# Decay counted from the start of each chunk of 128 tokens, the first unit's block loaded in three parts, and another PSUM bank for a 32-row step

## The chip, the cores and the metric

The kernel runs on one core of one Trainium2 chip. The metric is device time in microseconds, the median of three runs. Engines are called by their roles: TensorE (PE in the profile, PEld for its weight loads), VectorE (DVE), ScalarE (ACT), GpSimd (POOL), and SyncE (SP), which issues most of the DMAs. A kernel has one instruction queue for each engine, and each queue runs in order.

## The reference

Three layers follow each other. The first is retention: for batch 4, 8 heads, 576 tokens and 64 columns a head, with a decay gamma of its own for each head.

```python
scores = scale * np.matmul(q, k.transpose(0, 1, 3, 2))
gamma = 1.0 - 2.0 ** (-5.0 - np.arange(H))
Dmat = np.where(rel >= 0, gamma ** rel, 0.0)      # rel = row - column
out = np.matmul(scores * Dmat, v)
```

Its 2304 rows of 512 columns go through a mixture of 8 experts (512 to 1024, ReLU, 1024 to 512; each row to the expert with the largest gate logit, with a capacity), and its output through a second mixture of 8 experts, where rows whose skip score is not positive are passed on unchanged. All of it is float32.

## The kernel before

**Attention** (`attention`, from L137) works in 20 units: for each batch four units of two heads with the first 512 tokens, and a fifth (`tail`) with the last 64 tokens of all heads. Because gamma to the power of (row - column) is a product of a power for the row and one for the column, the queries are multiplied by gamma^row / 8 (`prep_q`, tile `qT`) and the values by gamma^-column (`prep_v`, tile `vh`). A main unit is four chunks of 128 tokens. Within a chunk the scores S = k q (`scores`, L219) are masked by a triangle on VectorE (`P`, L222) and multiplied by `vh` into the output O (`pv`, L263). What earlier chunks give comes through a state: `state` (L231) multiplies keys and `vh` of each chunk into one PSUM tile `kv`, whose pool has one buffer. ScalarE copies the first chunk's part (L239) and VectorE adds the other three one after another (L237). `inter` (L249) multiplies the queries with the state of the chunks before. The decay is counted from the start of the sequence, so the tables of queries have 576 columns for each pair of heads (tile `qt`): 128 are loaded, and ScalarE makes the others from them (`powers`, L205). For the first two units VectorE makes `qT` in four steps (L195, L198) from those 128. GpSimd makes `qT` of the others (L193), all `vh` but the first (L183), and both of the tails (L190, L181). The pool of `qT` and that of `vh` have three buffers.

**Order.** `round_(u)` puts the parts of neighbouring units together: prepare unit u + 1, a background slot, `inter(u - 1)`, a slot, `scores(u)`, `pv(u - 1)`, a slot, `state(u + 1)`, and the load of unit u + 5. TensorE runs in the order in which the code names the work, and from round 1 on GpSimd does too. In the first stretch, up to the end of round 0, VectorE and ScalarE also keep the written order; what is left, and VectorE, ScalarE and SyncE from round 1 on, is ordered by a planner, which simulates the program when it is built. The slots take the work of `tokens_out`: for a finished batch the gate logits (L346, copied out of PSUM at L348), their transposes `Lt` (L359), the router's chain of small VectorE operations with one exponential on ScalarE (L361 to L396, L449 to L481), the transposes of rows (L663) and their copies (L664). In the list of batch 1, `pick_first` (its count matmul `pf` is L502) chooses the expert that layer 1 begins with. GpSimd scatters the rows with indirect DMAs (L493).

**The loads.** SyncE issues them. For unit 0 these are keys and queries (512 KB), the 128 query columns of all pairs (256 KB), 56 table columns (28 KB), the keys and values by tokens (512 KB) and 260 more table columns (130 KB). Units 1 to 3 have one load of 1 MB each; the rest of the table follows unit 3. Five main blocks fit at once.

**The expert layers** come behind. First products (h, pool `psH` of two banks) are put through ReLU, and second products are summed over eight steps in four banks `y0` to `y3`. In layer 2, where the planner orders TensorE alone, an entry of 32 rows (`small1`, `small2`) works between entries 0 and 2. It sums its outputs `ys` (L903) in bank `y3`, which VectorE empties for entry 0 (L956), and ScalarE copies them out (`hold`, L1132).

Of the kernel before, what the change touches and what calls it, by code (L numbers as in the profile page):

```python
# [53 lines left out]
TAB0, TAB1 = 56, 316  # L54
# [6 lines left out]
def host_tables():  # L61
    gam = 1.0 - 2.0 ** (-5.0 - np.arange(H, dtype=np.float64))
    p = np.arange(128)
    vtab = np.zeros((128, 4, 5, 2))
    for h in range(H):
        for t in range(5):
            vtab[:, h // 2, t, h % 2] = gam[h] ** (-(128.0 * t + p))
    own = lambda j: np.repeat(gam[2 * j:2 * j + 2], 64)[:, None]
    qrow = np.stack([own(j) ** np.arange(128.0) / 8.0 for j in range(4)], axis=1)
    qg = np.stack([own(j) ** (128.0 * np.arange(1, 5)) for j in range(4)], axis=1)  # L70
    vtl = np.stack([[[gam[4 * j + 2 * a + h] ** (-(512.0 + t)) for h in range(2)] for a in range(2)] for j in range(2) for t in range(64)])
    one = np.ones((128, 1))
    cols = {
        "vtab": vtab.reshape(128, 40),
        "qg": qg.reshape(128, 16),
        "tri": p[:, None] <= p[None, :],
        "tri2": (p[:, None] <= p[None, :]) & (p[:, None] // 64 == p[None, :] // 64),
# [18 lines left out]
    return {"tab": np.ascontiguousarray(tab), "qrow": np.ascontiguousarray(qrow.astype(np.float32))}, off  # L96
# [40 lines left out]
def attention(g, hooks):  # L137
# [13 lines left out]
    def load(u):  # L151
# [10 lines left out]
        part = lambda c0, c1: nc.sync.dma_start(out=g.tab[:, c0:c1], in_=g.ia["tab"][:, c0:c1])  # L162
        if u == 0:
            nc.sync.dma_start(out=x[:, 0:1024], in_=src[:, 0:1024])
            nc.sync.dma_start(out=g.qt[:, :, 0:128], in_=g.ia["qrow"])
            part(0, TAB0)
            nc.sync.dma_start(out=x[:, 1024:], in_=src[:, 1024:])
            part(TAB0, TAB1)
        else:
            nc.sync.dma_start(out=x, in_=src)  # L170
        if u == 3:
            part(TAB1, g.tab.shape[1])
            g.small_loads()
        elif u == 10:
            g.clear(1)

    def prep_v(u):
        s = st[u]
        s.vh = g.wk.tile([128, 4, 2, DH], F32, tag="vh", name=f"vh{u}", bufs=3)
        if tail(u):  # L180
            nc.gpsimd.tensor_mul(s.vh[:, 0:2], s.v, g.vtl[:, :, :, None].to_broadcast([128, 2, 2, DH]))  # L181
        else:
            (nc.gpsimd if u else nc.vector).tensor_mul(s.vh, s.v, g.vtab[:, s.p, 0:4, :, None].to_broadcast([128, 4, 2, DH]))  # L183

    def prep_q(u):

        s = st[u]
        s.qT = g.wk.tile([128, 512], F32, tag="qT", name=f"qT{u}", bufs=3)
        if tail(u):
            nc.gpsimd.tensor_mul(s.qT[:, 0:256].rearrange("p (a j t) -> p a j t", a=2, j=2), s.q.rearrange("p (a j t) -> p a j t", a=2, j=2),  # L190
                                 g.qt[:, :, 512:576].rearrange("p (j a) t -> p a j t", a=2))
        elif u > 1:
            nc.gpsimd.tensor_mul(s.qT, s.q, g.qt[:, s.p, 0:512])  # L193
        else:
            nc.vector.tensor_mul(s.qT[:, 0:128], s.q[:, 0:128], g.qt[:, s.p, 0:128])  # L195
            for c in range(1, 4):
                cs = slice(128 * c, 128 * c + 128)
                nc.vector.scalar_tensor_tensor(out=s.qT[:, cs], in0=s.q[:, cs], scalar=g.qg[:, s.p, c - 1:c], in1=g.qt[:, s.p, 0:128],  # L198
                                               op0=ALU.mult, op1=ALU.mult)

    def powers(p):

        for c in range(1, 5):
            w = 128 if c < 4 else 64
            nc.scalar.activation(g.qt[:, p, 128 * c:128 * c + w], g.qt[:, p, 0:w], AF.Copy, scale=g.qg[:, p, c - 1:c])  # L205
# [18 lines left out]
    def state(u):  # L224
# [8 lines left out]
        s.st = [g.st3[main.index(u) % 2][:, c] for c in range(3)] + [g.st4[s.b % 2][:, s.p]]  # L233
        for c in range(4):
            x = kv[:, DH * c:DH * c + DH]
            if c:
                nc.vector.tensor_add(s.st[c], s.st[c - 1], x)  # L237
            else:
                nc.scalar.copy(s.st[c], x)  # L239
# [79 lines left out]
    with g.tc.manual_schedule(engines={T.PE, T.DVE, T.Activation}):  # L319
        prep_q(0)  # L320
        prep_v(0)
        scores(0)
        state(0)
        prep_q(1)
        prep_v(1)
        powers(2)
        powers(3)
        round_(0)
        powers(0)
        powers(1)  # L330
# [292 lines left out]
def tokens_out(g, b):  # L623
# [48 lines left out]
    if b == 1:  # L672
        return [logits, choose, rows[0], rows[1], g.r1.pick_first, rows[2], step, rows[3], rows[4], puts, lambda: g.puts.append(g.first)]
# [124 lines left out]
class Layer:  # L798
# [98 lines left out]
    def small2(self, pos, f, w):  # L897

        g, s = self.g, self.st[pos]
        if f == 0:  # L900
            s.y = [g.psY.tile([128, 512], F32, tag="y3", name=f"ys{pos}")[:, 0:128]]
# [523 lines left out]
def build(nc, tc, ia, oa, off, stage=99):  # L1425
# [4 lines left out]
    with ExitStack() as ctx:  # L1430
# [7 lines left out]
        tab = cp.tile([128, tw], F32, name="tab")  # L1438
# [6 lines left out]
        for n_, (o0, o1) in off.items():  # L1445
            setattr(g, n_, tab[:, o0:o1])
        g.tid1 = g.rid[:, 0:NT]
        g.vtab = g.vtab.rearrange("p (a t h) -> p a t h", a=4, t=5)
        g.qg = g.qg.rearrange("p (a c) -> p a c", a=4)
        g.vtl = g.vtl.rearrange("p (a h) -> p a h", a=2)  # L1450
# [40 lines left out]
        with ExitStack() as ac:  # L1491
# [9 lines left out]
            g.qt = ap.tile([128, 4, 576], F32, name="qt")  # L1501
# [11 lines left out]
            g.st3 = [ap.tile([128, 3, DH], F32, name=f"st3_{i}") for i in range(2)]  # L1513
# [50 lines left out]
```

## Time and profile before

| | us |
|---|---|
| median of 3 runs | 524.47 (523.34 to 529.84) |
| the profiled execution | 523.61 |
| its span, first to last instruction | 521.7 |
| TensorE busy | 498.2 |
| VectorE busy | 288.0 |
| ScalarE busy | 213.8 |
| GpSimd busy | 142.8 |

The span is shorter than the time of the execution by what lies around it. An engine counts as busy while an instruction of its own runs; waiting, branching and issuing DMAs do not count. A wait is put down to what ended it, written with an arrow.

### The profile page before, as it was taken

How to read it: one execution, taken by the hardware profiler on the slowest of the kernel's cores; microseconds unless marked ns; L12 is line 12 of the kernel's file. 1: busy time of each engine (PE TensorE's matmuls, PEld its weight loads, DVE VectorE, ACT ScalarE, POOL GpSimd, SP SyncE). 2: the span in 40 equal slices, each digit the busy share in tenths (PEclk: the TensorE clock that was granted, in tenths of full speed). 3: DMA queues.
4: the chain of work that ended last, by engine and by line, in shares of the span. 5: the costliest groups of instructions: out<-in, count | busy, mean ns of one | idle time of the engine just before them, and what ended most of it. 6: DMA issues, size and time to landing. Idle time of an engine off the chain costs nothing.

```text
span 521.7 us, 11984 instructions
## 1 busy us (share of the span) xinstructions
PE 498.2 (95%) x4411; PEld 464.2 (89%) x4411; DVE 288.0 (55%) x840; ACT 213.8 (41%) x432; POOL 142.8 (27%) x210
## 2 busy tenths in 40 slices
PE   7999798999999999999999999999999999999993
PEld 6877676798999999999999899999899889999992
DVE  4655748445365856667585857453657665522012
ACT  2332133324354746556474756332534524321120
POOL 1657465331222030412014150513110320110111
PEclk9999899999999999999999999999999999999997
DMA  8979664946997457584848563607869999988800
GB/s 308 405 231 383 211 173 155 323 134 187 297 287 229 137 166 204 190 229 132 244 128 252 162 223 123 174 11 195 283 207 298 323 302 270 290 269 274 288 24 33
DMA packets 90920, 114.15 MB, mean 219 GB/s; under 512 B 15685, under 2 KB 65861, under 8 KB 88933
## 3 DMA queue, kind: packets, MB, share of 16 engines
q1 hardware_dynamic: 84517, 99.23, 62.9%
q0 software_dynamic: 6336, 14.07, 7.2%
q8 instruction: 36, 0.59, 0.5%
q14 instruction: 31, 0.25, 0.2%
HBM read 97.99 MB, written 20.17 MB: 226 GB/s over the span
## 4 chain that ended last, share of the span: by engine, by line
PE 74%; DMA 10%; DVE 7%; issue 3%; SPq 2%; ACT 2%; POOL 1%; POOLq 0%; DVEq 0%; ACTq 0%
PE h L858 13%; PE y L934 9%; PE h L869 5%; PE h L870 5%; PE h L868 5%; PE y L938 5%; PE y L939 5%; PE y L937 5%; PE O L263 3%; PE S L219 3%; DMA rows<-xs 2%; PE y L931 2%; DMA xb<-xs 2%; PE yr L979 2%; PE O L249 2%
## 5 line engine op out<-in xcount | busy, mean ns | idle before, releaser
L786 DVE TENSOR_TENSOR lo<-r,hi 128x1024 fp32r<-128x1024 f32 x80 | 97.7, 1223 | 51.1 <-ACT hi L786 48.6
L786 ACT CAST hi<-r 128x1024 fp32r<-128x1024 f32 x80 | 83.6, 1047 | 35.6 <-PE y L938 20.1
L938 PE MATMUL y<-hl,hi 128*128 128x316 f32 (+7 forms) x256 | 76.3, 299 | 1.0 <-DVE hl L874 1.0
L939 PE MATMUL y<-hh,lo 128*128 128x316 f32 (+7 forms) x256 | 76.0, 298 | 0.0
L937 PE MATMUL y<-hh,hi 128*128 128x316 f32 (+7 forms) x256 | 74.8, 297 | 0.0
L493 POOL DMA_INDIRECT xs<-x2s,idx x20 | 23.3, 1164 | 166.9 <-DVE hl L874 46.9
L934 PE MATMUL y<-hh,r 128*128 128x176 f32 (+3 forms) x384 | 60.3, 300 | 0.0
L873 ACT ACTIVATE hh<-h 128x316 fp32r<-128x316 f32 (+8 forms) x72 | 29.2, 406 | 70.7 <-PE h L870 70.7
L934 PEld LDWEIGHTS y<-hh,r 128*128 128x128 f32 x384 | 55.0, 190 | 0.0
L874 DVE SCALAR_TENSOR_TENSOR hl<-h,hh 128x316 fp32r<-128x316 f32 (+8 forms) x72 | 32.3, 448 | 37.7 <-ACT hh L873 37.6
L938 PEld LDWEIGHTS y<-hl,hi 128*128 128x128 f32 x256 | 48.2, 188 | 1.6 <-DVE hl L874 1.6
L939 PEld LDWEIGHTS y<-hh,lo 128*128 128x128 f32 x256 | 48.3, 188 | 0.0
L937 PEld LDWEIGHTS y<-hh,hi 128*128 128x128 f32 x256 | 47.7, 188 | 0.2
L865 ACT ACTIVATE hh<-h 128x176 f32<-128x176 f32 (+3 forms) x48 | 14.6, 305 | 77.1 <-PE h L858 74.5
L1138 POOL DMA_INDIRECT out<-o,oi x13 | 16.7, 1285 | 101.8 <-DVE o L1213 69.8
L956 DVE COPY yt<-y 128x176 f32<-128x176 f32 (+11 forms) x28 | 10.5, 391 | 44.3 <-ACT yt L958 26.5
L222 DVE TENSOR_TENSOR P<-S,tab 128x512 f32<-128x512 f32 (+1 forms) x40 | 23.8, 632 | 13.5 <-PE S L219 13.4
L274 ACT COPY xT<-O 128x512 f32<-128x512 f32 x16 | 9.3, 584 | 35.2 <-PE O L263 35.2
L1138 POOL DMA_INDIRECT out<-x2r,si x20 | 21.3, 1066 | 6.1 <-issue 5.2
L858 PE MATMUL h<-x_0h,r 128*128 128x160 f32 (+1 forms) x128 | 22.7, 312 | 0.0
L219 PE MATMUL S<-qT,m 64*128 64x128 f32 x256 | 20.0, 295 | 2.4 <-DVE qT L195 1.6
L263 PE MATMUL O<-P,vh 128*64 128x128 f32 x288 | 21.9, 296 | 0.0
(617 smaller groups left out, 1183.7 us busy)
## 6 DMA issues: line engine op xcount, KB each, us to landing
r<-w1a SPq DMA_DIRECT2D x32, 512.0 KB, 4.9
r<-w2a SPq DMA_DIRECT2D x32, 512.0 KB, 5.6
r<-w1b SPq DMA_DIRECT2D x32, 512.0 KB, 5.9
r<-w2b SPq DMA_DIRECT2D x32, 512.0 KB, 5.6
m<-main SPq DMA_DIRECT2D x15, 1024.0 KB, 11.1
xb<-xs SPq DMA_DIRECT2D x12, 160.0 KB, 5.2
rows<-xs SPq DMA_DIRECT2D x7, 258.0 KB, 3.7
xb<-xs SPq DMA_DIRECT2D x12, 144.0 KB, 4.4
```

The source lines that it names most:

```text
L219: nc.tensor.matmul(S[hh][:, c], s.kT[hp, cs], s.qT[hp, cs], start=True, stop=True)
L263: nc.tensor.matmul(s.O[64 * hh:64 * hh + 64, 128 * c:128 * c + 128], s.vh[:, c, hh], s.P[:, hh, c], start=False, stop=True, skip_group_che ...
L786: high, low = lambda: nc.scalar.copy(hi, raw), lambda: nc.vector.tensor_sub(lo, raw, hi.bitcast(F32))
L858: nc.tensor.matmul(ps, w.r1[:, c, fc], s.xh[:, c, 0:C], start=(c == 0), stop=(c == 3))
L868: nc.tensor.matmul(ps, w.hi1[:, c, fc], s.xh[:, c, 0:C], start=(c == 0), stop=False)
L873: nc.scalar.activation(s.hh[f], ps, AF.Relu)
L874: nc.vector.scalar_tensor_tensor(out=s.hl[f], in0=ps, scalar=0.0, in1=s.hh[f].bitcast(F32), op0=ALU.max, op1=ALU.subtract)
L934: nc.tensor.matmul(y, w.r2[:, f % 2, dc], s.hh[f], start=a, stop=o)
L937: nc.tensor.matmul(y, wh, s.hh[f], start=a, stop=False)
L938: nc.tensor.matmul(y, wh, s.hl[f], start=False, stop=False)
L939: nc.tensor.matmul(y, wl, s.hh[f], start=False, stop=o)
L1138: r = g.nc.gpsimd.indirect_dma_start(out=g.oa["out"][:, :].rearrange("n (b d) -> (n b) d", b=parts), out_offset=IndirectOffsetOnAxis(ap=id ...
```

## The change

The decay is counted from the start of each chunk. `vh` of a main unit is the value times gamma^-p with p the row in its chunk, the same for all four chunks, so it has one scale a row and head: two ScalarE instructions, one a head, make it. `qT` takes the same 128 table columns for each chunk, in one product on VectorE (units 0 and 1) or GpSimd; `powers` and its ScalarE instructions go. The state is carried from chunk to chunk with gamma^128: ScalarE copies all four parts of `kv` out of PSUM times gamma^128 (tile `w`), and VectorE makes `state * gamma^128 + w` three times, in SBUF alone. The tail's product of queries becomes two.

Unit 0's block is loaded as queries, a first table part (268 columns with `vtab`, `g128`, the first pair's query columns and the triangle), keys, keys and values by tokens, and a second table part of 516 columns. The query table `qrow` is no longer a tensor of its own. In batch 1's list `pick_first` comes after four rows and no longer after two. `ys` is summed in a bank of the pool `psH`.

```diff
@@ -51,7 +51,7 @@
 GATE, TOK, VAL = 512, 513, 514
-TAB0, TAB1 = 56, 316
+TAB0, TAB1 = 268, 784
 F32_MAX = 192
@@ -61,19 +61,18 @@
     p = np.arange(128)
-    vtab = np.zeros((128, 4, 5, 2))
-    for h in range(H):
-        for t in range(5):
-            vtab[:, h // 2, t, h % 2] = gam[h] ** (-(128.0 * t + p))
     own = lambda j: np.repeat(gam[2 * j:2 * j + 2], 64)[:, None]
-    qrow = np.stack([own(j) ** np.arange(128.0) / 8.0 for j in range(4)], axis=1)
-    qg = np.stack([own(j) ** (128.0 * np.arange(1, 5)) for j in range(4)], axis=1)
-    vtl = np.stack([[[gam[4 * j + 2 * a + h] ** (-(512.0 + t)) for h in range(2)] for a in range(2)] for j in range(2) for t in range(64)])
+    qrow = np.stack([own(j) ** np.arange(128.0) / 8.0 for j in range(4)], axis=1).reshape(128, 512)
+    g128 = np.concatenate([own(j) ** 128.0 for j in range(4)], axis=1)
+    vtab = gam[None, :] ** (-p[:, None])
+    vtl = np.stack([[[gam[4 * j + 2 * a + h] ** (-float(t)) for h in range(2)] for a in range(2)] for j in range(2) for t in range(64)])
     one = np.ones((128, 1))
     cols = {
-        "vtab": vtab.reshape(128, 40),
-        "qg": qg.reshape(128, 16),
+        "vtab": vtab,
+        "g128": g128,
+        "qrow0": qrow[:, 0:128],
         "tri": p[:, None] <= p[None, :],
+        "qrows": qrow[:, 128:],
         "tri2": (p[:, None] <= p[None, :]) & (p[:, None] // 64 == p[None, :] // 64),
@@ -93,7 +92,7 @@
     tab = np.concatenate([c_.astype(np.float32) for c_ in cols.values()], axis=1)
-    return {"tab": np.ascontiguousarray(tab), "qrow": np.ascontiguousarray(qrow.astype(np.float32))}, off
+    return {"tab": np.ascontiguousarray(tab)}, off
@@ -159,17 +158,17 @@
         s.k, s.v = (x[:, o:o + 512].rearrange("p (c h d) -> p c h d", c=4, h=2) for o in (1024, 1536))
-        part = lambda c0, c1: nc.sync.dma_start(out=g.tab[:, c0:c1], in_=g.ia["tab"][:, c0:c1])
+        part = lambda c0, c1: nc.sync.dma_start(out=g.ta[:, c0:c1], in_=g.ia["tab"][:, c0:c1])
         if u == 0:
-            nc.sync.dma_start(out=x[:, 0:1024], in_=src[:, 0:1024])
-            nc.sync.dma_start(out=g.qt[:, :, 0:128], in_=g.ia["qrow"])
-            part(0, TAB0)
-            nc.sync.dma_start(out=x[:, 1024:], in_=src[:, 1024:])
+            for c0, c1 in ((512, 1024), (0, 512), (1024, 2048)):
+                nc.sync.dma_start(out=x[:, c0:c1], in_=src[:, c0:c1])
+                if c0 == 512:
+                    part(0, TAB0)
             part(TAB0, TAB1)
         if u == 3:
-            part(TAB1, g.tab.shape[1])
+            nc.sync.dma_start(out=g.tab, in_=g.ia["tab"][:, TAB1:])
             g.small_loads()
@@ -180,29 +179,20 @@
         else:
-            (nc.gpsimd if u else nc.vector).tensor_mul(s.vh, s.v, g.vtab[:, s.p, 0:4, :, None].to_broadcast([128, 4, 2, DH]))
+            for hh in range(2):
+                nc.scalar.activation(s.vh[:, :, hh], s.v[:, :, hh], AF.Copy, scale=g.vtab[:, 2 * s.p + hh:2 * s.p + hh + 1])
         if tail(u):
-            nc.gpsimd.tensor_mul(s.qT[:, 0:256].rearrange("p (a j t) -> p a j t", a=2, j=2), s.q.rearrange("p (a j t) -> p a j t", a=2, j=2),
-                                 g.qt[:, :, 512:576].rearrange("p (j a) t -> p a j t", a=2))
-        elif u > 1:
-            nc.gpsimd.tensor_mul(s.qT, s.q, g.qt[:, s.p, 0:512])
+            for j in range(2):
+                nc.gpsimd.tensor_mul(*(x[:, 0:256].rearrange("p (a j t) -> p a j t", a=2, j=2)[:, :, j] for x in (s.qT, s.q)),
+                                     g.qtail[j])
         else:
-            nc.vector.tensor_mul(s.qT[:, 0:128], s.q[:, 0:128], g.qt[:, s.p, 0:128])
-            for c in range(1, 4):
-                cs = slice(128 * c, 128 * c + 128)
-                nc.vector.scalar_tensor_tensor(out=s.qT[:, cs], in0=s.q[:, cs], scalar=g.qg[:, s.p, c - 1:c], in1=g.qt[:, s.p, 0:128],
-                                               op0=ALU.mult, op1=ALU.mult)
-
-    def powers(p):
-
-        for c in range(1, 5):
-            w = 128 if c < 4 else 64
-            nc.scalar.activation(g.qt[:, p, 128 * c:128 * c + w], g.qt[:, p, 0:w], AF.Copy, scale=g.qg[:, p, c - 1:c])
+            (nc.gpsimd if u > 1 else nc.vector).tensor_mul(s.qT.rearrange("p (c t) -> p c t", c=4), s.q.rearrange("p (c t) -> p c t", c=4),
+                                                           g.qrow[s.p][:, None, :].to_broadcast([128, 4, 128]))
@@ -230,13 +220,11 @@
                                  start=True, stop=True, skip_group_check=True)
-        s.st = [g.st3[main.index(u) % 2][:, c] for c in range(3)] + [g.st4[s.b % 2][:, s.p]]
-        for c in range(4):
-            x = kv[:, DH * c:DH * c + DH]
-            if c:
-                nc.vector.tensor_add(s.st[c], s.st[c - 1], x)
-            else:
-                nc.scalar.copy(s.st[c], x)
+        w, gm = g.wk.tile([128, 4, DH], F32, tag="kv", name=f"kvs{u}", bufs=3), g.g128[:, s.p:s.p + 1]
+        s.st = [w[:, 0]] + [g.st3[main.index(u) % 2][:, c] for c in range(2)] + [g.st4[s.b % 2][:, s.p]]
+        nc.scalar.activation(w, kv[:, 0:4 * DH].rearrange("p (c d) -> p c d", c=4), AF.Copy, scale=gm)
+        for c in range(1, 4):
+            nc.vector.scalar_tensor_tensor(out=s.st[c], in0=s.st[c - 1], scalar=gm, in1=w[:, c], op0=ALU.mult, op1=ALU.add)
@@ -323,11 +311,7 @@
         prep_v(1)
-        powers(2)
-        powers(3)
         round_(0)
-        powers(0)
-        powers(1)
     with g.tc.manual_schedule(engines={T.PE, T.Pool}):
@@ -670,7 +654,7 @@
     if b == 1:
-        return [logits, choose, rows[0], rows[1], g.r1.pick_first, rows[2], step, rows[3], rows[4], puts, lambda: g.puts.append(g.first)]
+        return [logits, choose, rows[0], rows[1], rows[2], rows[3], g.r1.pick_first, step, rows[4], puts, lambda: g.puts.append(g.first)]
     return [logits, choose, rows[0], rows[1], None, rows[2], step, rows[3]] + [None] * (b // 2) + [puts]
@@ -898,7 +882,7 @@
         if f == 0:
-            s.y = [g.psY.tile([128, 512], F32, tag="y3", name=f"ys{pos}")[:, 0:128]]
+            s.y = [g.psH.tile([128, 512], F32, tag="h", name=f"ys{pos}")[:, 0:128]]
         for b in range(4):
@@ -1435,7 +1419,7 @@
         tw = max(o[1] for o in off.values())
-        tab = cp.tile([128, tw], F32, name="tab")
+        tab = cp.tile([128, tw - TAB1], F32, name="tab")
         g.tab = tab
@@ -1443,11 +1427,9 @@
         for n_, (o0, o1) in off.items():
-            setattr(g, n_, tab[:, o0:o1])
+            if o0 >= TAB1:
+                setattr(g, n_, tab[:, o0 - TAB1:o1 - TAB1])
         g.tid1 = g.rid[:, 0:NT]
-        g.vtab = g.vtab.rearrange("p (a t h) -> p a t h", a=4, t=5)
-        g.qg = g.qg.rearrange("p (a c) -> p a c", a=4)
-        g.vtl = g.vtl.rearrange("p (a h) -> p a h", a=2)
         wg = cp.tile([128, 2, 4, 32], F32, name="wg")
@@ -1498,7 +1480,14 @@
             g.misc = ac.enter_context(tc.tile_pool(name="psX", bufs=2, space=PSUM))
-            g.qt = ap.tile([128, 4, 576], F32, name="qt")
+            ta = g.ta = ap.tile([128, TAB1], F32, name="ta")
+            for n_, (o0, o1) in off.items():
+                if o0 < TAB1:
+                    setattr(g, n_, ta[:, o0:o1])
+            o = off["qrow0"][0], off["qrows"][0] + 128
+            g.qtail = [ta[:, o[0]:o[0] + 512].rearrange("p (a w) -> p a w", a=2)[:, :, 0:64], ta[:, o[1]:o[1] + 256].rearrange("p (a w) -> p a w", a=2)[:, :, 0:64]]
+            g.qrow = [g.qrow0] + [g.qrows[:, 128 * j:128 * j + 128] for j in range(3)]
+            g.vtl = g.vtl.rearrange("p (a h) -> p a h", a=2)
             g.xtail = ap.tile([128, 4, DH], F32, name="xtail")
@@ -1510,7 +1499,7 @@
-            g.st3 = [ap.tile([128, 3, DH], F32, name=f"st3_{i}") for i in range(2)]
+            g.st3 = [ap.tile([128, 2, DH], F32, name=f"st3_{i}") for i in range(2)]
             g.st4 = [ap.tile([128, 4, DH], F32, name=f"st4_{i}") for i in range(2)]
```

## Rows read from the trace of the kernel before

**Rows 1.** Page, parts 1 and 4: busy time by engine; the chain by engine.

```profile
PE 498.2 (95%) x4411; PEld 464.2 (89%) x4411; DVE 288.0 (55%) x840; ACT 213.8 (41%) x432; POOL 142.8 (27%) x210
PE 74%; DMA 10%; DVE 7%; issue 3%; SPq 2%; ACT 2%; POOL 1%; POOLq 0%; DVEq 0%; ACTq 0%
```

**Rows 2.** Waits of TensorE, 0 to 130 us: total us, times, longest.

```profile
PE pf L502 <- DVE st L237: 2.8, 1, 2.8
PE kv L231 <- POOL vh L183: 1.6, 2, 1.0
PE S L219 <- DVE qT L195: 1.6, 1, 1.6
PE kv L231 <- DVE st L237: 1.5, 1, 1.5
PE S L219 <- DVE P L222: 0.8, 1, 0.8
```

**Rows 3.** Timeline at 366 us: start, us, engine line operation xcount [idle before <-releaser].

```profile
366.49 0.62 PE L903 MATMUL ys<-r,ht 128*32 128x128 f32 x10 [1.10 <-DVE yt L956]
```

**Rows 4.** Windows: us, busy by engine (instructions), PEclk (granted clock), DMA share, GB/s.

```profile
46.00:62.00 16.00, 12.23 (x196) 9.60 (x192) 11.05 (x37) 3.93 (x11) 11.28 (x15) 1.00 0.77 270
62.00:66.00 4.00, 4.00 (x41) 3.15 (x39) 1.78 (x7) 1.17 (x2) 0.61 (x1) 0.57 0.64 211
```

**Rows 5.** Timeline: VectorE operations with SBUF operands alone, and a GpSimd product.

```profile
6.72 0.87 DVE L198 SCALAR_TENSOR_TENSOR qT<-m,tab,qt 128x128 f32<-128x128 f32 x3
11.73 1.66 DVE L198 SCALAR_TENSOR_TENSOR qT<-m,tab,qt 128x128 f32<-128x128 f32 x3
54.00 3.39 DVE L382 TENSOR_TENSOR r1sh<-L,r1mx 128x40 f32<-128x40 f32 x1
56.29 1.04 POOL L183 TENSOR_TENSOR vh<-m,tab 128x512 f32<-128x512 f32 x1
77.77 3.00 DVE L466 TENSOR_TENSOR r2s<-oh,psh 128x32 f32<-128x32 f32 x1
```

**Rows 6.** Groups by shape, 0 to 100 us: busy us, mean ns, idle before, releasers.

```profile
L193 POOL TENSOR_TENSOR qT<-m,qt 128x512 f32<-128x512 f32 x14 | 17.8, 1274 | 7.9 <-issue 3.6 <-DMA m<-main 2.8 <-POOL vh L181 0.6
L183 POOL TENSOR_TENSOR vh<-m,tab 128x512 f32<-128x512 f32 x15 | 15.7, 1047 | 14.6 <-DMA m<-main 10.3 <-PE O L263 4.3
L205 ACT ACTIVATE qt<-qt,tab 128x128 f32<-128x128 f32 x12 | 3.9, 390 | 0.0
L205 ACT ACTIVATE qt<-qt,tab 128x64 f32<-128x64 f32 x4 | 1.3, 333 | 0.0
L239 ACT COPY st<-kv 128x64 f32<-128x64 f32 x16 | 3.4, 215 | 11.9 <-PE kv L231 11.6
L272 ACT COPY xtail<-O 128x256 f32<-128x256 f32 x2 | 0.7, 372 | 1.4 <-PE O L263 1.4
L237 DVE TENSOR_TENSOR st<-st,kv 128x64 f32<-128x64 f32 x48 | 10.5, 218 | 7.8 <-ACT st L239 6.9
```

**Rows 7.** Timeline of the start: first scores, third unit's q product and its state.

```profile
6.86 2.08 PE L219 MATMUL S<-qT,m 64*128 64x128 f32 x16 [1.61 <-DVE qT L195]
14.14 1.27 POOL L193 TENSOR_TENSOR qT<-m,qt 128x512 f32<-128x512 f32 x1 [1.42 <-DMA m<-main]
16.46 0.69 PE L231 MATMUL kv<-vh,m 128*64 128x64 f32 x16 [0.64 <-POOL vh L183]
```

**Rows 8.** Timeline: one unit's scores.

```profile
61.05 1.16 PE L219 MATMUL S<-qT,m 64*128 64x128 f32 x16
```

**Rows 9.** Timeline: TensorE behind a ScalarE copy; ScalarE behind VectorE.

```profile
28.33 0.42 PEld L359 LDWEIGHTS Lt<-ident,l 128*128 128x128 f32 x4 [0.20 <-ACT l L348]
57.42 0.24 ACT L383 ACTIVATE r1sh<-r1sh 128x40 f32<-128x40 f32 x1 [5.05 <-DVE r1sh L382]
```

**Rows 10.** Timeline: a unit's last state sum and its first use.

```profile
33.18 0.22 DVE L237 TENSOR_TENSOR st<-st,kv 128x64 f32<-128x64 f32 x1
36.83 0.87 PE L249 MATMUL O<-qT,st 64*64 64x128 f32 x12
```

## The prediction

> **What bounds the kernel now.** I read the page first, then who TensorE waits for, then the stages by windows, then the timeline around each wait. The page shows TensorE busy for 95% of the span and most of the chain that ended last lying on it, with VectorE at 55% and ScalarE at 41% [rows 1]. So only time in which TensorE stands still, or runs slowly, is to be had. Nearly all of it lies in the first 130 us, in five waits [rows 2]: 2.8 us before the count matmul pf, 1.6 us in two waits of a state product kv for its scaled values vh, which come from GpSimd, 1.6 us before the first scores, 1.5 us of one kv for VectorE's running sums, 0.8 us of scores for VectorE's masked products. A sixth, 1.1 us, lies in layer 2 before ys [rows 3]. The windows add something that no list of waits shows: from 62 to 66 us the granted clock is 0.57 on average, and 1.00 in the stretch before, which holds TensorE's longest wait [rows 4]. 0.57 over 4 us is 3.4 us at the lower level (1.2 GHz) and the rest at 2.4 GHz, so about 1.7 us of full-speed work were lost just after a 2.8 us standstill.
>
> **Why VectorE is late there.** A subtraction of 128x40 takes 3.39 us at 54.00 and a product of 128x32 takes 3.00 us at 77.77. The first ends within 0.1 us of the GpSimd product vh that runs from 56.29 to 57.33 [rows 5]. VectorE's mask products and sums, which read PSUM, keep their length throughout (the sums' mean is 218 ns over 48) [rows 6]. What is behind the stalled operation on VectorE is what pf, kv and S wait for.
>
> **The change, part by part.** The sum is made against the profiled execution: 523.6 us, of which 521.7 are span and 1.9 lie around it. The median of the runs shown, 524.47, is 0.9 above it.
>
> Scaled values. Fifteen GpSimd products of 1047 ns go, and the scaling products of q, 1274 ns each, stay [rows 6]. In their place come two ScalarE instructions of 128x256 a unit. The nearest form, a copy with a scale per partition, takes 390 ns for 128 columns and 333 for 64 [rows 6]; the slope gives 0.50 us for 256, so 1.0 us a pair. ScalarE's table powers (3.9 + 1.3 us) go, and the sixteen state copies of 215 ns become scaled copies of 128x256, about 372 ns by the unscaled copy of that size [rows 6]. ScalarE's net is 16 x 1.0 + 16 x 0.16 - 5.2 = +13.4 us on an engine that has room, but it takes them in its queue.
>
> Start, **-1.3 us**. Query and its table first, and one VectorE product for four, bring the first scores forward from 6.9 us. That in itself buys nothing: the bytes ahead of the third unit's block are the same within 2% (1438 KB before, 1416 after, by the diff's widths), the block lands at 14.14, and now GpSimd makes qT and then vh before kv starts at 16.46 [rows 7]. With vh on ScalarE from 14.14 on, kv can start at 15.2. Bounds: 0, if ScalarE's queue holds it back, and 2.0, if narrow pieces also bring the block forward.
>
> The wait at 49 us, **-1.0 us**: the second of the two waits for vh [rows 2]. Two row scatters, qT and then vh stand in GpSimd's queue there; vh is no longer in it. Bounds 0 and 1.0.
>
> pick_first two places later, **-2.8 us**. pf leaves its place right behind the router's chain. Ahead of it now stand two transposes of rows, a unit's scores (1.16 us [rows 8]), its outputs of as many matmuls, and the next state, over 3 us of work, while the chain itself loses a vh product of 1.05 us or two from its stall. What is late next there is the mask product for that unit, queued on VectorE behind the same chain; the outputs need it one stage later than pf needed the counts. Bounds 0.5 and 2.8. With the standstill goes the slow stretch behind it, **-1.7 us** (0 if another wait of that length appears).
>
> State sums, **-2.3 us**. kv's one bank is now read by a single ScalarE copy and is free at once, and no longer after three VectorE sums: the 1.5 us wait. The 0.8 us wait for the mask product goes because the stalled 77.77 product can end with qT, one vh product sooner [rows 2, 5]. Bounds 0.8 and 2.3.
>
> Layer 2's small step, **-1.1 us**: ys waits for VectorE to empty bank y3 [rows 3]; a bank of the first products is long empty. The copy that empties ys is needed only by the second following first product. Bounds 0 and 1.1.
>
> Together -10.2. Against it, **+2.0 us** on ScalarE. TensorE's transposes Lt start as soon as ScalarE's copy l ends and wait for it [rows 9], four times, once for each batch; a vh pair put ahead of that copy costs up to 1.0 us, and I take half, 4 x 0.5. Bounds: 0, and 0.5 in each of 16 units, 8.0. The same queue can hold vh behind the router's exponential, which sat idle 5.05 us for VectorE [rows 9]; the shorter stall bounds that, and it is in the 8.0.
>
> The new sums: **0**, by slack. They take a scalar and two SBUF operands, which the old ones (one operand in PSUM) did not. Three such VectorE operations took 0.87 us alone and 1.66 us beside a GpSimd product [rows 5], so up to one qT product (1.27 us) may be added to a unit's chain. But a unit's sums end at 33.40 and its first use starts at 36.83 [rows 10]: 3.4 us cover it in a plain round. The Trainium skill, "SBUF — State Buffer", section "Who interferes with whom", speaks against the change here: a VectorE instruction with two SBUF inputs contends with a GpSimd instruction that reads SBUF, and the later one blocks fully. By that rule the stalls above and the new exposure are the same thing; its trace side agrees (3.39 and 3.00 us), and it is the last rival below.
>
> Sum: 523.6 - 10.2 + 2.0 = **515.4**.
>
> **The rivals.**
> All of it closes: ScalarE's idle time takes the pairs, and the start gives 2.0. 523.6 - 10.9 = 512.7. For it: ScalarE's 41%. Against: Lt's tight wait. Chance 0.20.
>
> ScalarE's queue paces TensorE: every unit pays 0.5 us. 523.6 - 10.2 + 8.0 = 521.4. For it: vh, kv, the emptied O bank, row copies and l now share one queue in an order that the planner writes without knowing of the stalls. Against: its share. Chance 0.18.
>
> The change does less than it says: qT products come back to back once vh is out of GpSimd's queue, so VectorE's stall lasts as long, the mask product takes over as what TensorE waits for, and the slow clock stays. Then only start, 49 us and ys count: 523.6 - 3.4 = 520.2. For it: the stall at 54.00 spans a qT product as well. Chance 0.12.
>
> The other side, slower: the sums are locked out by qT. It decides once the sums' slack falls under 1.27 + 0.7 us, so that each unit's products with the state wait. Price 15 x 1.27 = 19.0 us; only the 3.4 us that need no VectorE stay: 523.6 + 19.0 - 3.4 = 539.2. Against: the 3.4 us of slack, and qT starting about when the second or third sum does. Chance 0.06. (By the Trainium skill, "SBUF — State Buffer", "Who interferes with whom", the lock falls at every overlap; whether it reaches TensorE is the slack's to say.)
>
> The forecast has the remaining 0.44.
>
> **How the numbers follow.** 515.4 is the likeliest case. The range 512 to 523 reaches from the case in which all closes, with 0.7 for the start's bound and the spread of the runs' low end, to the ScalarE case with the 0.9 by which the median stands over the profiled run and its own rounding; left out are the locked case and tails. About 2%, 10.5 us, is what a measurement of this kernel can tell from no change. Faster by that needs the case in which all closes and a little of the forecast: 0.25. Slower by that needs most of the lock: 0.05. Within: 0.70.
>
> **What would show it.** kv of the third unit near 15.2 us and its wait gone or put down to a DMA; no wait of pf and a granted clock of 1.00 throughout 46 to 66 us; no kv waiting for VectorE; the sums' mean near 0.25 us with a few over 1 us; ys without a wait; Lt's waits for l longer. The forecast is wrong if waits for ScalarE pass 4 us in all, if a state product waits for a sum, or if the later stages are reordered so that waits appear behind 130 us.

## The result and the profile after

| | before | changed |
|---|---|---|
| median of the runs made side by side | 524.77 us (11 runs, 523.34 to 530.30) | 521.51 us (11 runs, 519.55 to 522.82) |
| ratio, with its 95% interval | | 0.9916 [0.9890, 0.9942] |
| profiled execution, and its span | 523.61, 521.7 | 522.13, 520.3 |

The ratio is worth 4.4 us [3.0, 5.8] of 524.8. It is faster, clear of its interval though by under 2%, and by about half of what was forecast (8.2 us). The median lies inside the forecast's range of 512 to 523, near its slow end. The two profiled executions differ by only 1.5 us, so stages are read from the traces below and the verdict from the runs.

The page, parts 1 and 4, busy time by engine and the chain that ended last, answers to [rows 1]:

```profile
PE 498.9 (96%) x4411; PEld 463.7 (89%) x4411; DVE 284.6 (55%) x833; ACT 225.9 (43%) x448; POOL 129.1 (25%) x199
PE 87%; DVE 4%; DMA 3%; issue 2%; ACT 2%; SPq 0%; POOL 0%; DVEq 0%; POOLq 0%; ACTq 0%
```

TensorE's share of the chain is 87% now and was 74%; VectorE's fell to 4%. GpSimd is busy 13.7 us less and ScalarE 12.1 us more.

The waits of TensorE over the whole span (total us, times, longest), against [rows 2]:

```profile
PE kv L221 <- ACT vh L183: 4.0, 1, 4.0
...
PE M L330 <- ACT yt L942: 1.2, 1, 1.2
PE O L251 <- issue: 1.1, 2, 0.9
...
PE hs L873 <- issue: 0.6, 2, 0.4
PE O L237 <- ACT kvs L225: 0.6, 1, 0.6
...
```

The waits of pf, of kv on VectorE's sums and of S on the mask product are gone. In their place stands one wait of 4.0 us, and it is at the very start. The windows (us, busy by engine, granted clock, DMA share, GB/s) show what follows it, and that the slow stretch of [rows 4] is cured:

```profile
7.20:10.00 2.80, 0.03 (x2) 0.00 (x0) 1.29 (x2) 0.65 (x1) 0.00 (x0) 1.00 0.98 387
10.00:16.80 6.80, 5.03 (x50) 4.36 (x52) 1.46 (x4) 2.83 (x7) 1.27 (x1) 0.50 1.02 416
46.00:62.00 16.00, 16.00 (x239) 12.20 (x237) 9.61 (x36) 8.97 (x21) 9.30 (x13) 1.00 0.84 303
62.00:66.00 4.00, 4.00 (x61) 3.37 (x61) 2.82 (x13) 1.64 (x3) 1.31 (x2) 1.00 0.71 256
```

From 7.2 to 10 us TensorE does next to nothing, and from 10 to 16.8 us its granted clock is 0.50 (1.2 GHz). The timeline of the start, against [rows 7], says why the standstill is so long:

```profile
9.35 1.28 ACT L183 ACT_TABLE_LOAD   x1 [9.35 <-DMA m<-main]
10.65 0.91 ACT L183 ACTIVATE vh<-m,ta 128x256 f32<-128x256 f32 x2
5.61 1.62 PE L209 MATMUL S<-qT,m 64*128 64x128 f32 x16 [0.36 <-DVE qT L194]
15.25 1.27 POOL L194 TENSOR_TENSOR qT<-m,ta 128x512 f32<-128x512 f32 x1 [13.93 <-DMA m<-main]
11.21 1.51 PE L221 MATMUL kv<-vh,m 128*64 128x64 f32 x16 [3.97 <-ACT vh L183]
18.33 1.03 PE L221 MATMUL kv<-vh,m 128*64 128x64 f32 x16
```

The first unit's keys and values land at 9.35 us. Only then does ScalarE load its activation table, 1.28 us, and then scale the values; the first kv starts at 11.21 (9.21 before), the third unit's at 18.33, where 15.2 was forecast and 16.46 was before. The third unit's block lands at 15.25 us, seen at the GpSimd product that waits for it, and landed at 14.14 before. But the third kv has no wait in front of it: TensorE was still busy with the work of the first two units.

How late the same matrix products start in the changed kernel, by two traces matched product by product (changed minus before; a step is the change of this lag within a stretch):

| stretch | lag at its end | step | forecast for it |
|---|---|---|---|
| start, to 25 us | +2.62 | +2.6 | -1.3 |
| kv's wait at 49 us | +1.43 | -1.2 | -1.0 |
| router products L at 52 and 72 us | | +0.7, +0.4 | +2.0 in four places |
| pick_first and the clock, 57 to 68 us | -2.21 | -4.4 | -4.5 |
| state sums and S, 78 to 88 us | -4.74 | -2.9 | -2.3 |
| probability products O at 91 us | -3.12 | +1.6 | none |
| 100 to 355 us | -1.60 | +1.5 | none |
| layer 2's small step | -1.30 | +0.3 | -1.1 |

A step under 1 us in one pair of traces says little by itself: at 25 us the kernel before and a run of it with the same start differ by 0.9 us.

### The profile page after: what moved, and what is told of

The parts are those of the page before. It is cut to its first block, busy times and chain, and to the rows that moved or that the text cites. A ratio compares the mean times of both kernels' runs of the same rounds, so it can differ in the third digit from the quotient of the medians.

```text
span 520.3 us, 11967 instructions
## 1 busy us (share of the span) xinstructions
PE 498.9 (96%) x4411; PEld 463.7 (89%) x4411; DVE 284.6 (55%) x833; ACT 225.9 (43%) x448; POOL 129.1 (25%) x199
## 4 chain that ended last, share of the span: by engine, by line
PE 87%; DVE 4%; DMA 3%; issue 2%; ACT 2%; SPq 0%; POOL 0%; DVEq 0%; POOLq 0%; ACTq 0%
PE h L842 13%; PE y L918 9%; PE h L854 7%; PE h L853 7%; PE h L852 7%; PE y L922 6%; PE y L923 6%; PE y L921 6%; PE O L251 4%; PE S L209 4%; PE O L237 3%; PE yr L963 3%; PE y L915 2%; PE xps L647 2%; PE kv L221 2%
## 5 line engine op out<-in xcount | busy, mean ns | idle before, releaser
L849 ACT ACTIVATE hh<-h 128x176 f32<-128x176 f32 (+3 forms) x48 | 14.7, 306 | 75.7 <-PE h L842 73.1
L212 DVE TENSOR_TENSOR P<-S,ta 128x512 f32<-128x512 f32 (+1 forms) x40 | 23.9, 629 | 12.3 <-PE S L209 9.0
L194 POOL TENSOR_TENSOR qT<-m,ta 128x512 f32<-128x512 f32 x14 | 18.0, 1285 | 25.4 <-DMA m<-main 15.2
```

## The experiments

Each ratio below is to the kernel before, run in the same batch, with its 95% interval; microseconds are that ratio applied to 524.8. The first question was whether the start alone explains the missing 4 us.

**The changed kernel again**, as a control.

> The changed kernel once more, as a control. Both theories: the ratio to before stays within 0.989 to 0.994, the first kv starts at 11.2 +- 0.3 us after a standstill of about 4 us. Open: the stall of 1.1 us that the first profile shows at 90.7 to 92.3 us on all engines, with no releaser. If it belongs to the kernel it comes back at the same matmuls; if it is chance it does not.

Measured 0.9935 [0.9907, 0.9962]. Its start is the same: first kv at 11.49 us, a granted clock of 0.5 from 9.95 to 16.77. The standstill near 91 us is there again, 0.96 us before the same products; it is taken up below.

**The table load ahead of everything.** One ScalarE copy of a 128x1 constant is put first, so that the load has no transfer to wait for.

```diff
+        nc.scalar.copy(g.tiny, g.zero[:, 0:1])
         prep_q(0)
         prep_v(0)
```

> The changed kernel with a ScalarE copy of 128x1 ahead of everything, so that ScalarE's table load has no DMA to wait for. Theory (the table load of 1.28 us stands behind the wait for unit 0's block, and the standstill of 4.0 us then halves the clock): first kv at 9.9 us, third kv 1.3 us earlier (17.0), or near 15.5 if the shorter standstill of 2.7 us keeps the clock at 1.00; ratio 0.986 to 0.989. Rival (the pieces of the load alone are to blame): first kv not before 10.9, ratio 0.991 as it is.

Measured 0.9897 [0.9868, 0.9927]. The timeline:

```profile
0.75 1.28 ACT L308 ACT_TABLE_LOAD   x1 [0.75 <-PEq L1548]
10.05 1.51 PE L221 MATMUL kv<-vh,m 128*64 128x64 f32 x16 [2.85 <-ACT vh L183]
17.78 1.02 PE L221 MATMUL kv<-vh,m 128*64 128x64 f32 x16
```

The load now lies in idle time and the first kv comes 1.16 us sooner. But TensorE still stands still for 2.85 us, its clock is 0.5 from 8.74 to 15.57 us, and the third kv gains only 0.55. Two more traces with the changed kernel's start have that kv at 18.45 and 17.90, so most of the gain may be spread. The forecast held for the first kv, not for the third (17.0 or 15.5), and the ratio is just above its range. The Trainium skill, "ScalarE: Activation LUTs", section "What ACT_TABLE_LOAD costs", gives 1283 ns for the load, which the trace shows, and 2.66 us with the drain of a switch; here the first activation starts 1.30 us after the load does.

**And TensorE kept busy.** As the last, with nine warm-up matmuls of a zero tile between the first scores and the first kv.

```diff
         scores(0)
+        for i in range(9):
+            nc.tensor.matmul(ps[:, 0:128], g.zero, g.zero, start=True, stop=True)
         state(0)
```

> As the kernel with the early table load, and nine more warm-up matmuls between the first scores and the first kv, so that TensorE does not stand still. Theory: granted clock 1.00 from 7 us on, first kv at 9.9, third kv near 15.5, ratio 0.983 to 0.987. Rival (the arrival of blocks two and three sets the third kv, not the clock): third kv within 0.3 us of the kernel with the table load alone, and no gain over it.

Measured 0.9859 [0.9833, 0.9886], 7.4 us below before. The timeline of the start, and a window of it:

```profile
9.70 1.08 PE L221 MATMUL kv<-vh,m 128*64 128x64 f32 x16 [0.40 <-ACT vh L183]
14.75 0.91 ACT L183 ACTIVATE vh<-m,ta 128x256 f32<-128x256 f32 x2 [0.30 <-DMA m<-main]
15.31 1.08 PE L221 MATMUL kv<-vh,m 128*64 128x64 f32 x16 [0.32 <-ACT vh L183]
```

```profile
10.00:16.80 6.80, 5.78 (x99) 4.73 (x100) 3.80 (x8) 3.66 (x9) 1.34 (x1) 1.00 1.02 411
```

The first kv moves by 0.35 us, the third by 2.5: the difference is the clock, 1.00 throughout. The third kv stands at 15.31, and 15.2 was forecast. So the forecast's figure for the start needs the full clock that the changed kernel does not have. That it is met so closely is luck: the block came to ScalarE at 14.75 us and not at 14.14, and kv followed 0.56 us later and not 1.0. With TensorE in time, the block's landing is what the third kv waits for.

**The old order of the first loads** (keys and queries in one transfer), with the early table load.

```diff
-            for c0, c1 in ((512, 1024), (0, 512), (1024, 2048)):
+            for c0, c1 in ((0, 1024), (1024, 2048)):
```

> As the kernel with the early table load, and unit 0's keys and queries in one load of 512 KB again, ahead of the first table part. Theory (the narrower pieces bring the block of keys and values 0.9 us later): block at 8.5 instead of 9.35 us, first scores at 6.0 to 6.9, first kv at 9.0 to 9.3, third kv 0.5 to 0.9 earlier than with the table load alone. Rival (the block lands when its bytes' turn comes, whatever the cuts): first kv at 9.9 as with the table load alone, first scores later, no gain.

Measured 0.9887 [0.9850, 0.9924]. The values land at 7.80 us, 1.7 sooner than with the three loads, where 0.9 was forecast, and the first kv starts at 8.36. The third unit's block is 1.7 us sooner as well (13.49 for 15.17). In all the traces the first values come at 9.0 to 9.6 us and the third block at 14.9 to 15.5 with three loads, at 7.5 to 8.5 and 13.2 to 14.1 with two. Yet the clock still falls, by a window of it:

```profile
9.10:19.40 10.30, 9.74 (x94) 8.39 (x92) 4.64 (x10) 3.94 (x9) 2.54 (x2) 0.50 0.99 393
```

Two standstills of 0.77 and 1.17 us were enough here, and the lower level lasted 10.2 us. The third kv, 17.53, gained 0.25 us of the 1.7 (0.5 to 0.9 was forecast): TensorE came to it late, and not the block.

**Start mended**: early table load, old order of the loads, ten warm-up matmuls for eight, and five more behind the first scores.

```diff
-    for i in range(8):
+    for i in range(10):
...
         scores(0)
+        for i in range(5):
+            nc.tensor.matmul(ps[:, 0:128], g.zero, g.zero, start=True, stop=True)
```

> The changed kernel with its start mended: ScalarE's table load ahead of everything, keys and queries of the first unit in one load, ten warm-up matmuls instead of eight, and five more between the first scores and the first state. Theory (the lost start is the standstill of TensorE, the table load and the lower clock that follows): granted clock 1.00 from 6 us on, first state product near 8.4 us, third near 14.5 (between 14.3 and 15.3), 3.0 to 4.5 us below the changed kernel, ratio 0.983 to 0.986. Rival (the third unit's block, which lands near 14.7 us, sets the third state product whatever stands before it): third at 15.2 to 15.4 and no better than the run with nine warm-up matmuls, ratio 0.986 to 0.988. Second rival (a start gained is given back by the row transfers near 80 us): third near 14.5 and a ratio of 0.989 or more.

Measured 516.43 us median against 525.84, ratio 0.9804 [0.9773, 0.9835]: the best of all, 10.3 us below before. The timeline and the window:

```profile
8.69 0.69 PE L221 MATMUL kv<-vh,m 128*64 128x64 f32 x16
13.51 0.91 ACT L183 ACTIVATE vh<-m,ta 128x256 f32<-128x256 f32 x2 [0.33 <-DMA m<-main]
14.07 1.08 PE L221 MATMUL kv<-vh,m 128*64 128x64 f32 x16 [0.31 <-ACT vh L183]
```

```profile
10.00:16.80 6.80, 6.42 (x104) 5.35 (x104) 4.96 (x11) 4.04 (x9) 1.93 (x2) 1.00 1.02 398
```

The third kv is 4.3 us sooner than in the changed kernel, and 4.3 us is the lead at 80 us too: nothing of it is given back in the middle, and the second rival falls. The ratio and the third kv are better than the theory's ranges. The first rival falls by its figures, but its mechanism is there: kv starts 0.56 us after ScalarE gets the block, as in the run with nine warm-up matmuls. The old order of loads brings that block at 13.5 us and not at 14.7, so order, early table load and warm-up matmuls each have a part in the 4.3 us.

The next three take the middle apart.

**pick_first in its old place**, everything else as changed.

> The changed kernel with the first expert's step (pick_first) back in its old place, after the second row instead of after the fourth. Theory (the place is worth the wait and the clock): the matmul of pick_first stands still again, about 2.8 us (0.5 to 2.8), TensorE's granted clock falls below 0.8 in 62:66, and the time is 2.8 to 4.5 us above the changed kernel's: a ratio to the kernel before of 0.997 to 1.001. Rival (with the sums off GpSimd the router's operations are no longer held up, so its result is in time in either place): no wait over 0.5 us at pick_first, clock 1.00 in 62:66, ratio 0.991 to 0.994 as the changed kernel.

Measured 0.9903 [0.9873, 0.9932]. The theory fell and the rival stands (its ratio is a shade lower than forecast): in its old place pf waits for nothing, and the clock stays up (a line of its timeline, and a window).

```profile
59.50 0.27 PE L486 MATMUL pf<-C,onesr 128*128 128x8 f32 x1
```

```profile
62.00:66.00 4.00, 4.00 (x57) 3.27 (x58) 3.01 (x11) 2.16 (x4) 2.09 (x3) 1.00 0.95 331
```

**pick_first in its new place alone**, in the kernel before:

```diff
-        return [logits, choose, rows[0], rows[1], g.r1.pick_first, rows[2], step, rows[3], rows[4], puts, lambda: g.puts.append(g.first)]
+        return [logits, choose, rows[0], rows[1], rows[2], rows[3], g.r1.pick_first, step, rows[4], puts, lambda: g.puts.append(g.first)]
```

> The kernel before with one edit alone: pick_first moved two places later. Theory (the place): no wait at pick_first, granted clock 1.00 in 62:66, 2.8 to 4.5 us less than before: ratio 0.991 to 0.995. Rival (the wait only passes to the next thing that VectorE and GpSimd hold up, since the 3.39 us and 3.00 us stalls of VectorE stay): other waits of TensorE of together 2 us or more appear between 58 and 80 us, ratio 0.997 or above. What it leaves of the changed kernel's gain is then the part of the sums, the values and the bank.

Measured 0.9964 [0.9938, 0.9990], 1.9 us. The wait and the slow clock go here too (lag -4.67 at 68 us, of which 0.9 came from the start), but it does not keep them: TensorE then waits at 66 to 100 us, partly for mask products behind a VectorE operation that is still held up (its timeline, then its waits). The ratio lies between the theory's range and the rival's, and the waits between 58 and 80 us come to 1.7 us where the rival had 2 or more, so each is right in part:

```profile
73.29 2.82 DVE L369 TENSOR_TENSOR r2e<-r2e,tab 128x32 f32<-128x32 f32 x1
```

```profile
PE O L263 <- issue: 0.9, 1, 0.9
PE O L263 <- DVE P L222: 0.8, 1, 0.8
PE S L219 <- DVE P L222: 0.6, 1, 0.6
PE L L346 <- ACT xT L274: 0.3, 1, 0.3
```

So either the place or the rest of the change cures pf's wait. That it is the values off GpSimd in particular, as the rival has it, no run takes apart; the next one bears on it.

**The values back on GpSimd**, everything else as changed.

```diff
-            for hh in range(2):
-                nc.scalar.activation(s.vh[:, :, hh], s.v[:, :, hh], AF.Copy, scale=g.vtab[:, 2 * s.p + hh:2 * s.p + hh + 1])
+            (nc.gpsimd if u else nc.vector).tensor_mul(s.vh, s.v, g.vtab[:, None, 2 * s.p:2 * s.p + 2, None].to_broadcast([128, 4, 2, DH]))
```

> The changed kernel with the scaling of the values back on GpSimd (one operation a unit, VectorE for the first unit) instead of two operations of ScalarE. Theory (the move to ScalarE pays in the middle and costs at the start): the wait of the kv matmuls on GpSimd's values comes back near 49 us (1.0 to 1.6 us), the state's wait near 80 us partly (0.8 to 2.3), against 0.5 to 1.1 us less at the start, since the table load no longer stands ahead of the first values: 1 to 3.4 us above the changed kernel, ratio 0.994 to 0.998. Rival (ScalarE's 12 us of added work is itself a price, forecast at 2.0 us): 1 to 3 us below the changed kernel, ratio 0.986 to 0.990, and the 1.6 us that TensorE loses near 91 us is gone.

Measured 1.0027 [1.0005, 1.0050]: 5.8 us above the changed kernel, more than the theory's 3.4, and slower than before; the rival, a gain, falls. Its start is 1.57 us better, so with the new sums the move to ScalarE is worth more than 5 us in the middle. One state sum in its timeline shows the price:

```profile
53.01 4.43 DVE L226 SCALAR_TENSOR_TENSOR st<-kvs,ta 128x64 f32<-128x64 f32 x1
53.68 1.27 POOL L193 TENSOR_TENSOR qT<-m,ta 128x512 f32<-128x512 f32 x1
54.91 1.04 POOL L182 TENSOR_TENSOR vh<-m,ta 128x512 f32<-128x512 f32 x1
56.09 1.27 POOL L193 TENSOR_TENSOR qT<-m,ta 128x512 f32<-128x512 f32 x1
59.05 0.66 PE L646 MATMUL xps<-ident,xT 128*128 128x128 f32 x4 [1.90 <-DVE L L344]
```

A sum of 0.28 us took 4.43, for as long as GpSimd's operations followed one another (the last of them, a vh, starts at 57.31), and TensorE waited 1.90 us for the reduction queued behind it. Ten of the 48 sums took over 0.8 us in this kernel, three in the changed one.

**The bank of ys alone**: the mended kernel with the 32-row step's outputs back in bank y3.

> The run with the mended start, and layer 2's 32-row step summing its outputs in its old bank again (y3 in place of the bank h). Theory (the old bank costs the wait that was read from the trace of before, 1.10 us at the step's first output product): a wait of about 1.1 us at ys on VectorE's yt comes back, the profiled span is 0.5 to 1.1 us longer from there on, ratio to the kernel before 0.981 to 0.983. Rival (TensorE stands still there in any bank, 0.4 to 0.6 us with no releaser at hs or ys, as in the changed kernel and in the mended one): the step from 355 to 375 us takes as long as before within 0.3 us, ratio 0.980 to 0.981.

Measured 0.9822 [0.9778, 0.9867], which cannot be told from the mended kernel's. The trace can be read closer. The wait is back as forecast:

```profile
361.74 0.62 PE L890 MATMUL ys<-r,ht 128*32 128x128 f32 x10 [1.10 <-DVE yt L943]
```

Against the mended kernel the lag goes from +1.79 before the step to +2.39 behind it, a step of 0.6 us: the mended kernel itself stands still for 0.38 us in ys with no releaser that the profile shows. Against the two further traces with the mended start and the new bank (the next two runs) it is 0.7 and 1.0 us. But two traces that both have the old bank, the kernel before and the one with pick_first moved, differ by 1.2 us in the same stretch. The wait is the bank's; what it is worth in time is not settled between nothing and about 1 us.

**The standstill near 91 us.** Two edits meant to move the first experts' weight loads out of that stretch (two rounds later; or two loads of eight).

> The run with the mended start, and the first experts' weight loads (512 KB each, eight of them) asked for two rounds later, some 9 us, than in it. Theory (the standstill of TensorE of 0.7 to 1.1 us at the probability products near 88 us comes from the burst of these loads): no standstill over 0.15 us at those products, 0.5 to 0.9 us less at 95 us; what the late weights then cost at the first expert (its first product near 99 us) is 2 to 6 us more and read apart. Rival (it belongs to the instructions, whatever is being loaded): 0.5 to 1.1 us of standstill at the same products, within 0.3 us of their time without the edit. The total is not the test: ratio 0.980 to 0.992.

> The run with the mended start, and only two of the first experts' eight weight loads of 512 KB asked for at 79 us; the other six are left to the stage of the experts. Theory (the standstill at the probability products near 87 us comes from the burst of these loads): the DMA share falls below 0.5 between 84 and 90 us and those products show no standstill over 0.2 us in all. Rival (it belongs to the instructions there, whatever is being loaded): 0.6 to 1.1 us of standstill at the same products. The time as a whole, 5 us or more longer since the experts then wait for weights, is not the test.

Neither moved them: all eight are still issued from 78.6 us and from 79.1 us on, as in the mended kernel (78.70). The order of SyncE's work is the planner's, and the round did not set that time. Neither theory was tested. What the runs give is the mended kernel twice more (0.9821 [0.9774, 0.9868]; 517.63 in one run), with the standstill at the same unit's products:

```profile
88.11 0.68 PE L251 MATMUL O<-P,vh 128*64 128x128 f32 x8 [0.97 <-issue]
```

## Why the prediction was wrong

**The step that failed is "Start, -1.3 us".** It said that with vh on ScalarE from 14.14 on, "kv can start at 15.2". The trace has 18.33, and the lag of 2.62 us stays to 45 us: a miss of 3.9, in the wrong direction. The step asked only when the third unit's block lands and how soon its values are scaled. It left out when TensorE would come to that kv. In the kernel before only 0.64 us of wait stood there [rows 7]; ahead of it TensorE was busy to 15.82 us with the second unit's scores:

```profile
14.66 1.16 PE L219 MATMUL S<-qT,m 64*128 64x128 f32 x16
```

To start at 15.2 that work had to move forward, and it moved back. The step passed over what the changed order does to the first unit: three transfers for two bring its values 0.9 us later (9.35 for 8.46), the table load that lay idle at 0.75 us moves behind that landing (1.28 us), and "query and its table first" makes TensorE finish the scores sooner and then stand still for 3.97 us. The scores start 1.25 us sooner, the first kv 2.0 us later. "The block lands at 14.14" failed too, with nearly the same bytes ahead of it: it landed at 15.25.

The work after the standstill ran at 1.2 GHz to 16.85 us. That is no loss against the kernel before, whose first unit ran at the same pace; the trace of before has no record of the granted clock ahead of 14.35 us, and its windows print 1.00 there, but the products tell the pace. The sixteen probability products of the first unit before, in the changed kernel at a clock of 0.50, and in the run with nine warm-up matmuls at 1.00:

```profile
12.12 1.97 PE L263 MATMUL O<-P,vh 128*64 128x128 f32 x16
14.76 1.97 PE L251 MATMUL O<-P,vh 128*64 128x128 f32 x16
12.34 1.09 PE L251 MATMUL O<-P,vh 128*64 128x128 f32 x16
```

But the clock stands between the changed kernel and 15.2: kept up, it moved the third kv by 2.5 us. That a slow stretch follows a long standstill was in [rows 4], and the forecast used it at 62 us but not here. The kernel with the mended start undoes all of this (the three loads, the late table load, the standstill) and gains 5.9 us on the changed one by the ratios.

With this term alone put right the forecast's -8.2 would be -4.3, and the runs show -4.4. That closeness is luck. The other steps of the table add up to -4.0 where the forecast had -6.9, and the whole trace is 1.3 us ahead, not 4.4. Two traces of the changed kernel agree within 0.5 us to 250 us and are 2.7 us apart at 355, so the rest lies in how single executions differ there.

**The wait at 49 us** went, -1.2 for -1.0.

**pick_first and the clock**: the size was right in the whole (-4.4 for -4.5), its cause only in part. The place alone takes the wait away in the kernel before, but keeps 1.9 us of the time; with the rest of the change the old place does as well. The forecast booked to the place what the rest would have done without it.

**State sums and S**: -2.9 for -2.3, no wait of kv on VectorE left. One router operation is still held up, 1.24 us at 78.61, for 3.00 before [rows 5].

**ScalarE's queue**: +1.1 for +2.0. It falls at the router, as the forecast had it, but on another wait. At 52 us the sixteen products L take 1.90 us, for 1.28 before:

```profile
52.02 1.90 PE L330 MATMUL L<-xT,wg 128*32 128x320 f32 x16
```

ScalarE's copy of the outputs that they read runs beside them, from 52.75 to 53.12 us; before, it was done at 49.43, ahead of the first product. The +0.4 at 72 us falls on L too, whose weight loads wait 0.5 us for the same copy. Lt, which the forecast named, waits no longer than before. The rival in which it paces TensorE gave 521.4, near the measured 521.51, by accident: the lag rises at two router products and not in every unit, and putting the values back costs 5.8 us. The forecast's mark, waits for ScalarE over 4 us in all, is passed (4.0, 1.2 and 0.6 us), by the one at the start; the 1.2, in layer 2, was 1.1 before.

**The new sums at 0 by slack** held: 3 of 48 sums took over 1 us, each beside a qT product on GpSimd (the first from 17.79 to 19.07 us); their mean is 0.36 us, where about 0.25 was forecast. Two of them in the timeline:

```profile
17.87 1.27 DVE L227 SCALAR_TENSOR_TENSOR st<-kvs,ta 128x64 f32<-128x64 f32 x1 [3.07 <-ACT kvs L225]
44.42 1.72 DVE L227 SCALAR_TENSOR_TENSOR st<-st,ta,kvs 128x64 f32<-128x64 f32 x2
```

The list of waits names no product of TensorE that waits for them. The rule from the Trainium skill, "SBUF — State Buffer", "Who interferes with whom", on which the slow rival stood, agrees with the 4.43 us above. The kernel with the values on GpSimd is that rival come true in the small: the same sums are free or dear by what else GpSimd has in its queue.

**Layer 2's bank**: the wait went, as forecast, and comes back with the old bank. The 1.1 us did not follow: the changed kernel's step is +0.3, with 0.6 us of standstill without a releaser in its place, and the run with the old bank leaves the size open.

**Not foreseen, and open.** TensorE stands still for 0.7 to 1.2 us in the probability products of one unit near 91 us, and the timeline of the changed kernel has no releaser:

```profile
90.89 0.55 PE L251 MATMUL O<-P,vh 128*64 128x128 f32 x6 [0.19 <-issue]
92.33 0.67 PE L251 MATMUL O<-P,vh 128*64 128x128 f32 x7 [0.89 <-issue]
```

The traces of the changed kernel and of all eleven runs have it, that of the kernel before does not. The run with the old sums and values and the new place of pick_first has it too, and so has the one with the new sums and values and the old place, so neither is needed for it. What sets it off was not found. Nor was the drift of +1.5 us between 100 and 355 us settled; its steps differ from profile to profile. From 200 to 355 us TensorE waits 2.1 us for VectorE in the changed kernel and 1.3 in the one before, which is a part of it. How a larger step comes about is seen once, in the control's trace: at 307 and 308 us TensorE waits 0.65 and 0.93 us in the experts' products, and the granted clock is 0.54 from 310 to 313.7.

## What to carry to other kernels

When a change moves the first transfers, follow the first unit of every engine to its first instruction: what else stood idle there (a table load) now stands in the way, and what TensorE finishes sooner it spends standing still. A standstill has to be priced with the clock behind it wherever it falls, and a few matmuls of zeros in it can be worth more than an earlier transfer. Two edits that cure the same wait don't add: ask of each what is left of it when the other is made.

## What the runs showed of the hardware

In the changed kernel the granted clock fell to the lower level at 10.02 us, in a standstill that began at 7.23. In the run with the early table load and the old order of loads it fell too, at 9.11 us, after standstills of 0.77 and 1.17 us, and stayed there for 10.2 us; the run with nine warm-up matmuls and the one with the mended start, with no standstill over 0.6 us there, kept 1.00. At the lower level sixteen probability products took 1.97 us, at the upper 1.09. In the kernel before they took 1.97 too at 12.12 us, where its trace has no record of the clock. The first unit's block in three loads brought the third unit's block at 14.9 to 15.5 us, in two loads at 13.2 to 14.1, with the bytes ahead of it within 2%. A VectorE operation that reads two operands in SBUF was held up for 4.43 us while GpSimd's operations followed one another, to the start of the ninth, and not for the length of one of them.
